# Which PSUM bank each of the last four output tiles takes

## The chip, the cores and the metric

The kernel runs on one core of one Trainium2 chip. The metric is the device time of one execution in microseconds (us). The time given is the median of three runs. One further execution was taken with the hardware profiler on; its rows are what is read below.

## The reference, cut to what matters

A block of attention feeds a feed-forward block (FFN). The attention keeps, for each of 768 positions, 96 local and 8 global keys. Its output is `x`, 3072 tokens by 512. The FFN takes the largest of three projections and projects back:

```
scores = scale * q @ k.T + bias            # (4, 8, 768, 64): batch, heads, positions, head size
a = softmax(where(keep, scores, -1e9));  attn = a @ v
x = attn.transpose(0, 2, 1, 3).reshape(3072, 512)
h = maximum(maximum(x @ w1, x @ w2), x @ w3)   # (3072, 768)
out = h @ w_out                                # (3072, 512), float32
```

## The kernel before, in words

**Tiles and chunks.** The 3072 tokens are 24 tiles of 128. The FFN works on chunks of two or four tiles (`SIZES`, line 88); the last chunk, number 6, has four tiles, 512 tokens. The hidden 768 columns are six blocks `f` of 128.

**Order.** The kernel is a list of small units written out by hand (`SCHEDULE`, lines 24 to 86). Every engine gets its instructions in that order and runs them in order; semaphores make it wait where it reads what another engine writes, or writes what another still reads. A unit's name is a letter and its numbers; `@n` gives the slot of a ring of buffers that it takes. Those that matter here:

- `Fc.f.j@n` (line 379): four matmuls of chunk `c`, block `f`, weight matrix `j`. The result is a 128 x 512 float32 tile `h` in slot `n` of the PSUM ring "h". The ring has four slots, each a bank.
- `fc.f.j` (lines 393 to 398) reads such a tile out: for `j` = 0 a copy into a bf16 tile `h01` (line 393), for `j` = 1 a maximum with it in place (line 395), for `j` = 2 the last maximum into slice `f` of the tile `ht` (line 398). With `.1` behind it, a `j` = 0 copy runs on VectorE (DVE); the maxima always do.
- `Oc.t` (line 403) is the second projection of one output tile: six matmuls, one for each `f`, that add up in one PSUM tile `po`, also in the ring "h". Each reads slice `f` of `ht` and slice `f` of `wo`.
- `wo` and the three `w123` tiles are filled earlier by casts, slice by slice (`W`, line 464, and `Q`, line 472).
- `E@2` (`u_E`) is the end: the second projection of the last chunk's four tiles, their copies out of PSUM (line 408, ScalarE, ACT, all but one) and their stores (line 409).

**The end.** `u_E` takes banks from the ring "h" six times through its helper `bank`. Tiles 0 and 1 get one bank each. TensorE (PE) runs blocks 0 to 4 of tile 0, then blocks 0 to 4 of tile 1, then block 5 of tile 0 and block 5 of tile 1. Tile 2 follows with all six blocks. Tile 3 comes in three pieces of 256, 128 and 128 columns, each in a bank of its own. That is 36 matmuls: 18 of 512 columns, 6 of 256 and 12 of 128. The stores of the first five results are issued by SyncE (SP), the last by ACT.

**The units just ahead.** The last of the schedule reads

```
s3.1 s5.0 s5.3 F6.2.2@2 F6.5.0@3 f6.4.2.1 f6.2.2.1 F6.0.2@1 f6.3.2.1 f6.0.2.1
F6.5.2@2 F6.5.1@0 f6.5.0.1@4 f6.5.1.1 f6.5.2.1 E@2
```

So when `u_E` begins, the four banks of the ring hold these tiles, in the order in which DVE reads them out: `F6.0.2` in bank 1, `F6.5.0` in bank 3, `F6.5.1` in bank 0, `F6.5.2` in bank 2. PE has computed `F6.5.2` ahead of `F6.5.1`, but DVE reads `F6.5.1` first. The slices 0 to 4 of `ht` are complete with the read-out of `F6.0.2`; slice 5 is complete with that of `F6.5.2`.

Before the change, `bank` counts on from the slot of `E@2`: its six calls give banks 2, 3, 0, 1, 2, 3.

Of the kernel before, what the change touches and what calls it, by code (L numbers as in the profile page):

```python
# [12 lines left out]
FP32 = mybir.dt.float32  # L13
# [73 lines left out]

SIZES = [4, 2, 2, 4, 4, 4, 4]
RINGS = {'r': 7, 'rv': 3, 'qb': 3, 'qkT': 4, 'sp': 2, 'h': 4, 'P': 8, 'xb': 4, 'xT': 3, 'wst0': 3, 'wst1': 3, 'ht': 2, 'h01': 5, 'rz': 4}


@with_exitstack
def kernel(
# [13 lines left out]
    nc = tc.nc  # L107
    B, H, S, D = q.shape
    NG = int(n_global)
# [4 lines left out]
    NT = S // 128  # L114
# [16 lines left out]
    pools = {}  # L131
    for name in RINGS:
        space = {"space": bass.MemoryType.PSUM} if name in ("sp", "h") else {}
# [3 lines left out]
    def ring(name, slot, shape, dtype, label):  # L137
        assert 0 <= slot < RINGS[name]
        return pools[name].tile(shape, dtype, name=label, tag=f"{name}{slot}")
# [22 lines left out]
    def words(ap):  # L162
        return ap.bitcast(mybir.dt.int32)
# [12 lines left out]
    def va(T):  # L176
        b, t = divmod(T, NT)
        return va_first[b % 2] if t == 0 else va_ring[(T - b - 1) % len(va_ring)]
# [88 lines left out]

    def u_V(slot, T, how):
        b, t = divmod(T, NT)
        for e in range(2):  # L270
            rows = slice(64 * e, 64 * e + NG // 2)
            if how == 2:
                copies[how](words(va(T)[rows]), words(va(b * NT)[rows]))  # L273
            else:
                copies[how](va(T)[rows], va(b * NT)[rows])
# [125 lines left out]
    def f2_mm(po, c, tt, fs, cols=slice(0, DM)):  # L401
        for f in fs:
            nc.tensor.matmul(po, ht[c][:, f, tt * 128:(tt + 1) * 128], wo[:, f, cols],  # L403
                             start=(f == 0), stop=(f == NF - 1))

    def f2_out(po, ost, c, tt, copy, cols=slice(0, DM), dma=nc.sync):
        T = chunks[c][tt]
        copy(ost, po)  # L408
        dma.dma_start(out=out[T * 128:(T + 1) * 128, cols], in_=ost)
# [14 lines left out]
    def u_E(slot):  # L424
        n = len(chunks[last])
        h, o = [0], [0]

        def bank(w):
            h[0] += 1
            return ring("h", (slot + h[0] - 1) % RINGS["h"], [128, w], FP32, "po")  # L430

        def stage(w):
            o[0] += 1
            name = ("wst0", "wst1")[o[0] % 2]
            return ring(name, o[0] // 2 % RINGS[name], [128, DM], FP32, "ost")[:, 0:w]

        po = [bank(DM) for _ in range(min(2, n - 1))]
        for tt, p in enumerate(po):
            f2_mm(p, last, tt, range(NF - 1))
        for tt, p in enumerate(po):  # L440
            f2_mm(p, last, tt, [NF - 1])
            f2_out(p, stage(DM), last, tt, nc.scalar.copy)
        for tt in range(2, n - 1):
            p = bank(DM)
            f2_mm(p, last, tt, range(NF))
            f2_out(p, stage(DM), last, tt, nc.scalar.copy)
        for lo, hi, copy, dma in ((0, 256, nc.scalar.copy, nc.sync), (256, 384, nc.vector.tensor_copy, nc.sync),
                                  (384, 512, nc.scalar.copy, nc.scalar)):
            p = bank(hi - lo)
            f2_mm(p, last, n - 1, range(NF), slice(lo, hi))  # L450
            f2_out(p, stage(hi - lo), last, n - 1, copy, slice(lo, hi), dma)
# [52 lines left out]
    def u_R(slot):  # L504
# [6 lines left out]
        nc.vector.tensor_copy(rbase[:, 0], rel[:, 1])  # L511

    units = {"l": u_l, "c": u_c, "v": u_v, "x": u_x, "y": u_y, "X": u_X, "G": u_G, "V": u_V, "S": u_S,
             "e": u_e, "m": u_m, "B": u_B, "K": u_K, "A": u_A, "n": u_n, "t": u_t, "u": u_u, "Z": u_Z,
             "F": u_F, "f": u_f, "O": u_O, "o": u_o, "s": u_s, "E": u_E, "w": u_w, "W": u_W, "q": u_q,
             "Q": u_Q, "D": u_D, "d": u_d, "R": u_R}
    with tc.manual_schedule():
        todo = SCHEDULE.split()
        for u in todo[:2] + [None] + todo[2:]:
# [3 lines left out]
            code, _, slot = u.partition("@")  # L523
# [34 lines left out]
```

## Time and profile before

| | |
|---|---|
| median of three runs | 179.37 us (179.29 to 179.99) |
| the profiled execution's own time | 179.93 us |
| its span, first to last instruction | 178.2 us |
| mean granted TensorE clock | 0.997 |
| PE busy with matmuls | 168.9 us, 95% of the span |
| DVE busy | 129.7 us, 73% |
| ACT busy | 107.6 us, 60% |
| second projection (line 403) | 34.0 us of PE, 156 matmuls |

The span is 1.73 us shorter than the execution's own time. In the profile's rows a group gives line, engine, operation, the tiles written and read, and a count; then busy time, the mean of one, and the idle time of the engine just ahead of them with what ended most of it. Rows of a timeline begin with the start and the duration in us. The chain of waits follows the last instruction back to whatever released each step. Matmuls are pipelined: one of 512 columns is shown as 0.38 us long while the next starts 0.216 us after it, so a run of n such matmuls shows as (n - 1) x 0.216 + 0.38 us.

### The profile page before, as it was taken

What the parts mean: (1) busy time and instruction counts of PE and PEld (TensorE: products, weight loads), DVE (VectorE), ACT (ScalarE), POOL (GpSimd) and SP (SyncE); (2) the same over time, 40 slices, a digit from 0 to 9 for tenths busy, and PEclk for the clock granted to TensorE, in tenths of its full rate; (3) what the DMA queues carried; (4) which work ended last, traced back from release to release, by engine and by line L of the source; (5) the groups of instructions that cost most, each with busy time, mean ns of one, the idle gap of its engine ahead of it and who ended that gap; (6) DMA issues with size and microseconds to landing.
All of it is one profiled execution on the core that took longest, in us unless ns stands there. A gap on an engine that the chain in (4) does not pass through costs nothing.

```text
span 178.2 us, 3903 instructions
## 1 busy us (share of the span) xinstructions
PE 168.9 (95%) x1525; PEld 94.6 (53%) x1525; DVE 129.7 (73%) x258; ACT 107.6 (60%) x166; POOL 45.6 (26%) x72
## 2 busy tenths in 40 slices
PE   7889999999999999999989999999999999999692
PEld 2456644567875867645345554644445464444242
DVE  6578849887787969576999568998668984355800
ACT  5988989666999768845759587426154823120022
POOL 3049755517053570000203601122001040000000
PEclk9999999999999999999999999999999999999998
DMA  4999999999999997499999899998980153460006
GB/s 144 351 292 314 365 371 323 342 297 332 299 263 130 163 259 144 91 347 290 198 314 224 155 162 289 269 147 257 219 169 3 42 137 60 177 235 0 4 21 216
DMA packets 66627, 37.49 MB, mean 210 GB/s; under 512 B 24624, under 2 KB 61360, under 8 KB 66608
## 3 DMA queue, kind: packets, MB, share of 16 engines
q1 hardware_dynamic: 66464, 37.17, 84.7%
q8 instruction: 12, 0.20, 0.4%
q10 hardware_dynamic: 144, 0.07, 0.1%
q14 instruction: 7, 0.06, 0.1%
HBM read 25.17 MB, written 6.29 MB: 177 GB/s over the span
## 4 chain that ended last, share of the span: by engine, by line
PE 77%; DMA 8%; ACT 5%; DVE 4%; issue 2%; POOL 1%; SPq 1%; ACTq 0%
PE h L379 45%; PE po L403 18%; PE sp L295 6%; DMA qkT<-qb 4%; DMA rawk<-in_k_dram 3%; PE op L337 3%; PE op L340 2%; ACT wmask L324 2%; ACT P L302 2%; PE tp L233 1%; PE tpq L227 1%; POOL va L273 1%; ACT qkT L241 1%; PE xtp L364 1%; SPq L195 1%
## 5 line engine op out<-in xcount | busy, mean ns | idle before, releaser
L379 PE MATMUL h<-xT,w 128*128 128x512 bf16 (+1 forms) x504 | 99.5, 349 | 0.1
L379 PEld LDWEIGHTS <-w 128*128 128x128 bf16 x504 | 47.3, 98 | 41.8 <-issue 0.7
L302 ACT ACTIVATE P<-sp 128x1024 bf16<-128x1024 f32 (+1 forms) x48 | 43.8, 953 | 14.7 <-PE sp L295 14.6
L403 PE MATMUL po<-wo,ht 128*128 128x512 bf16 (+2 forms) x156 | 34.0, 363 | 1.5 <-DVE ht L398 1.5
L395 DVE TENSOR_TENSOR h<-h,h 128x512 bf16<-128x512 bf16 (+1 forms) x42 | 25.0, 606 | 10.4 <-PE h L379 7.5
L311 DVE TENSOR_TENSOR P<-P,wmask 128x1024 bf16<-128x1024 bf16 x38 | 26.6, 708 | 7.9 <-ACT P L302 7.8
L398 DVE TENSOR_TENSOR ht<-h,h 128x512 bf16<-128x512 bf16 (+1 forms) x42 | 26.5, 644 | 4.4 <-PE h L379 3.4
L393 ACT CAST h<-h 128x512 bf16<-128x512 f32 (+1 forms) x24 | 12.7, 538 | 21.6 <-PE h L379 21.4
L213 POOL CAST va<-rawv 64x512 bf16<-64x512 f32 x20 | 15.1, 757 | 29.4 <-DMA rawv<-in_v_dram 19.2
L403 PEld LDWEIGHTS <-ht 128*128 128x128 bf16 x156 | 13.9, 98 | 15.8 <-DVE ht L398 2.0
L349 DVE TENSOR_TENSOR xb<-op,rz 128x512 bf16<-128x512 f32 x24 | 16.6, 691 | 0.8
L393 DVE CAST h<-h 128x512 bf16<-128x512 f32 (+1 forms) x18 | 10.7, 596 | 8.6 <-PE h L379 8.4
L295 PE MATMUL sp<-qkT 64*128 64x128 bf16 x352 | 14.5, 218 | 1.8 <-ACT qkT L241 0.8
L273 POOL COPY va<-vaf 4x260 int32<-4x260 int32 x20 | 9.1, 454 | 24.8 <-PE op L340 23.5
L295 PEld LDWEIGHTS <-qkT 64*128 64x128 bf16 x352 | 10.0, 94 | 10.0 <-issue 6.1
L418 ACT COPY ost<-po 128x512 f32<-128x512 f32 x15 | 8.8, 590 | 8.3 <-PE po L403 8.3
L337 PEld LDWEIGHTS <-P 128*128 128x128 bf16 x192 | 12.5, 97 | 2.5 <-issue 0.5
L337 PE MATMUL op<-va,P 128*128 128x65 bf16 x160 | 12.6, 193 | 0.0
L340 PEld LDWEIGHTS <-P 128*128 128x128 bf16 x160 | 10.5, 97 | 1.6
L478 PE MATMUL wp<-zeros 128*128 128x256 bf16 (+1 forms) x43 | 9.8, 360 | 1.2 <-DVE cap L496 1.2
L340 PE MATMUL op<-va,P 128*128 128x65 bf16 x128 | 9.9, 193 | 0.4 <-POOL va L273 0.4
L408 ACT COPY ost<-po 128x512 f32<-128x512 f32 (+2 forms) x5 | 2.3, 481 | 12.3 <-PE po L403 12.2
(69 smaller groups left out, 128.7 us busy)
## 6 DMA issues: line engine op xcount, KB each, us to landing
rawv<-in_v_dram SPq DMA_DIRECT2D x12, 512.0 KB, 7.5
out_dram<-ost SPq DMA_DIRECT2D x23, 256.0 KB, 2.5
rawk<-in_k_dram SPq DMA_DIRECT2D x10, 512.0 KB, 7.4
rawq<-in_q_dram SPq DMA_DIRECT2D x10, 512.0 KB, 7.3
wst<-in_moe_w_dram SPq DMA_DIRECT2D x3, 1024.0 KB, 10.3
wst<-in_moe_w_dram SPq DMA_DIRECT2D x3, 512.0 KB, 8.1
wost<-in_moe_w_out_dram SPq DMA_DIRECT2D x3, 512.0 KB, 6.5
rawqk<-in_k_dram SPq DMA_DIRECT2D x2, 512.0 KB, 5.0
```

The costliest lines, as they stand in the source:

```text
L213: copies[how](heads(va(T))[64 * e:64 * e + 64, :, 0:D], src)
L295: nc.tensor.matmul(sp[:, hh, j2, ds], qT(T - ds, 1)[hsl, jp], qT(T, 0)[hsl, jp], start=not how, stop=True, skip_group_check=True)
L302: nc.scalar.activation(P[:, :, 0:n], sps[T, g].rearrange("p a b d n -> p (a b) d n")[:, :, 0:n], AF.Exp, bias=0.0, scale=scale)
L311: mul(P, P, wmask[:, g, :, 0:2])
L337: nc.tensor.matmul(o, P[:, i, 0], heads(va(T))[:, h], start=True, stop=(t == 0), skip_group_check=True)
L340: nc.tensor.matmul(o, P[:, i, 1], heads(va(T - 1))[:, h], start=False, stop=True, skip_group_check=True)
L349: nc.vector.tensor_tensor(out=x.rearrange("p (g h) d -> p g h d", g=2), in0=o4[:, :, :, 0:64], in1=rz[:, :, :, None].to_broadcast([128, 2, ...
L379: nc.tensor.matmul(ps, w123[f // 2][:, j, dm, (f % 2) * 128:(f % 2) * 128 + 128], xT[c][:, dm], start=(dm == 0), stop=(dm == 3))
L393: copies[how](h01, ps)
L395: nc.vector.tensor_max(h01s[c, f], h01s[c, f], ps)
L398: nc.vector.tensor_max(dst, h01s[c, f].rearrange("p (t e i) -> p t e i", e=2, i=64), ps.rearrange("p (t e i) -> p t e i", e=2, i=64))
L403: nc.tensor.matmul(po, ht[c][:, f, tt * 128:(tt + 1) * 128], wo[:, f, cols], start=(f == 0), stop=(f == NF - 1))
```

## The change

`u_E` no longer counts on from its slot. Its calls of `bank` run through a fixed list of banks, 1, 3, 0, 2, and around again:

| | tile 0 | tile 1 | tile 2 | tile 3, columns 0 to 255 | 256 to 383 | 384 to 511 |
|---|---|---|---|---|---|---|
| before | 2 | 3 | 0 | 1 | 2 | 3 |
| changed | 1 | 3 | 0 | 2 | 1 | 3 |

```diff
+LAST_BANKS = (1, 3, 0, 2)
+
...
     def u_V(slot, T, how):
         b, t = divmod(T, NT)
+        if how == 3:
+            dst, src = (va(x).rearrange("(e i) w -> e i w", e=2)[:, 0:NG // 2] for x in (T, b * NT))
+            nc.sync.dma_start(out=dst, in_=src)
+            return
         for e in range(2):
...
         def bank(w):
             h[0] += 1
-            return ring("h", (slot + h[0] - 1) % RINGS["h"], [128, w], FP32, "po")
+            return ring("h", LAST_BANKS[(h[0] - 1) % len(LAST_BANKS)], [128, w], FP32, "po")
```

The new branch in `u_V` is for units `V` whose last number is 3. The schedule has sixteen units `V`, all with 0, 1 or 2 there, so the branch issues nothing. The schedule itself, the order of all instructions and the staging tiles of the output are as before.

## The prediction

> **What bounds the kernel now.** I read the page first, for the busy times and the costliest groups.
>
> ```profile
> PE 168.9 (95%) x1525; PEld 94.6 (53%) x1525; DVE 129.7 (73%) x258; ACT 107.6 (60%) x166; POOL 45.6 (26%) x72
> ...
> PE 77%; DMA 8%; ACT 5%; DVE 4%; issue 2%; POOL 1%; SPq 1%; ACTq 0%
> ...
> L403 PE MATMUL po<-wo,ht 128*128 128x512 bf16 (+2 forms) x156 | 34.0, 363 | 1.5 <-DVE ht L398 1.5
> ```
>
> PE is busy for 95% of the span and carries 77% of the chain, so time is won only where PE stands still. The second projection has 1.5 us of idle time ahead of it in all its 156 matmuls, and one releaser has ended all of that: DVE's last maximum into `ht`. To see where this is I took the chain of waits from 160 us to the end:
>
> ```profile
> 159.98 7.93 PE h L379 x36
> 167.91 0.02 issue
> 167.93 0.70 DVE h L395
> 168.63 0.02 issue
> 168.66 0.73 DVE ht L398
> 169.39 0.05 issue
> 169.44 5.40 PE po L403 x36
> 174.84 0.03 ACTq L408
> 174.86 0.04 issue
> 174.90 0.27 ACT ost L408
> ```
>
> It is one stop. PE finishes its last first-projection block at 167.91, then the chain leaves PE for two DVE instructions (`f6.5.1` and `f6.5.2`), and PE goes on at 169.44 with all 36 matmuls of `u_E` in a row. Nothing but PE and the last copy is on the chain from there on. The timeline of this stretch shows who is busy meanwhile:
>
> ```profile
> 166.21 0.73 DVE L398 TENSOR_TENSOR ht<-h,h 128x512 bf16<-128x512 bf16 x1
> 166.83 0.68 DVE L393 CAST h<-h 128x512 bf16<-128x512 f32 x1
> 167.93 0.69 DVE L395 TENSOR_TENSOR h<-h,h 128x512 bf16<-128x512 bf16 x1 [0.43 <-PE h L379]
> 168.66 0.72 DVE L398 TENSOR_TENSOR ht<-h,h 128x512 bf16<-128x512 bf16 x1
> ...
> 169.44 5.38 PE L403 MATMUL po<-wo,ht 128*128 128x512 bf16 x36 [1.54 <-DVE ht L398]
> 172.02 1.07 ACT L408 COPY ost<-po 128x512 f32<-128x512 f32 x2 [11.42 <-PE po L403]
> 172.63 2.84 SPq L409 DMA_DIRECT2D out_dram<-ost  x5
> ```
>
> By their order on DVE the four rows are the read-outs `f6.0.2` (bank 1, done at 166.94), `f6.5.0` (bank 3, 167.51), `f6.5.1` (bank 0, 168.62) and `f6.5.2` (bank 2, 169.38). The first matmul of `u_E` writes bank 2, which is the bank read out last.
>
> **The change part by part.** Nothing is added or removed: the same 36 matmuls, five ACT copies, one DVE copy and six stores. What moves is the time from which each bank may be written.
>
> *Start of tile 0.* Its bank is now 1, free at 166.94, almost a us before PE ends the last block. The matmuls of blocks 0 to 4 also need slices 0 to 4 of `ht`, complete at the same 166.94. The question is whether a matmul waits for its slice or for the whole tile `ht`, whose slice 5 comes at 169.38. In the row above both reasons (bank 2 and slice 5) end together, so it can't say. The timeline from 20.8 to 26.5 us can:
>
> ```profile
> 20.90 1.03 POOL L464 CAST w<-wst 128x1024 bf16<-128x1024 f32 x1 [0.23 <-DMA wst<-in_moe_w_dram]
> ...
> 22.80 1.03 POOL L464 CAST w<-wst 128x1024 bf16<-128x1024 f32 x1
> ...
> 23.37 3.40 PE L379 MATMUL h<-xT,w 128*128 128x512 bf16 x15
> ...
> 25.30 1.05 ACT L464 CAST w<-wst 128x1024 bf16<-128x1024 f32 x1
> ```
>
> These three casts fill the slices `j` = 1, 0 and 2 of one weight tile (`W0.1.2`, `W0.0.2`, `W0.2.0`), and all three stand ahead of `F0.0.1` in the schedule. `F0.0.1` reads slice 1 alone and starts at 23.37, before the second cast ends (23.83) and 1.9 us before the third begins. So a matmul waits for the slice it reads. `ht[:, f]` is cut in the same way.
>
> PE can therefore go straight on. A run of three matmuls takes 0.81 us on the timeline (shown length of the last 0.38, so 0.216 from start to start). The last of the 36 in the chain starts at 167.91 - 0.02 - 0.38 = 167.52 (nearly the end shown, less its length), so tile 0 starts at 167.52 + 0.22 = 167.73 instead of 169.44: **1.70 us earlier**. The idle time of 1.54 us is the lower bound of this; the other 0.16 is the pipelined part of the last matmul, 0.38 - 0.22, which the next one overlaps when nothing holds it.
>
> *Tile 1*, bank 3: free at 167.51, needed after five matmuls at 167.73 + 5 x 0.216 = 168.81. No wait. *Block 5 of tile 0* needs slice 5. PE comes to it after ten matmuls, 167.73 + 10 x 0.216 = 169.89. The slice was let go at 169.44 in the rows. Cover left: 0.45 us. This is the next thing that would be late; without it, each us that DVE takes longer is a us at the end. *Tile 2*, bank 0, is free at 168.62 and needed after 169.89. No wait.
>
> *Tile 3.* Its first piece takes bank 2, read out at 169.38 and needed some four us after PE's start. The second takes bank 1, the third bank 3, and there ACT's copies of tiles 0 and 1 must be over; before, the same two copies freed banks 2 and 3 for the same two pieces. They run from 172.02 to 173.09 (two in 1.07 us), and PE reaches these pieces 4.5 us after its start, at 173.98 (18 matmuls of 0.216, then 6 of half their width and half their time: 169.44 + 3.89 + 0.65). They move with the matmuls, so their 0.9 us of cover stays. No new wait.
>
> *What follows the matmuls.* ACT has been idle for 11.42 us before its first copy and DVE for 5.1 us before its one, so both can come 1.70 us earlier. SP's queue holds only these five stores; the view by stages gives a DMA share of 0.01 from 160 to 167.9 us and 0.00 up to 169.44, so the stores meet no other transfer. The closing part, 174.90 to 178.2 (last copy, store and the end of the program, 3.3 us), hangs on the last copy and moves whole.
>
> *Clock.* Whether the gap costs clock, or its end would give some back:
>
> ```profile
> 160.00:167.90 7.90, 7.89 (x36) 3.32 (x34) 5.21 (x8) 0.59 (x1) 0.00 (x0) 1.00 0.01 2
> 167.90:169.44 1.54, 0.00 (x1) 0.01 (x1) 1.41 (x2) 0.00 (x0) 0.00 (x0) 1.00 0.00 0
> 169.44:174.90 5.46, 5.38 (x36) 3.02 (x36) 0.29 (x1) 2.03 (x4) 0.00 (x0) 1.00 0.26 98
> ```
>
> The column behind the engines is the granted clock: 1.00 ahead of the gap, in it and after it. I put nothing for it. *The unused branch in `u_V`* issues nothing: 0.
>
> **The sum** is -1.70 us. The profiled execution would be 179.93 - 1.70 = 178.23 us, with a span of 176.5. The median of the runs is 0.56 us below that execution; the gap is at PE's end in either, so I take the same difference from the median: 179.37 - 1.70 = **177.67 us**, 0.95% less.
>
> **Rivals.** *1. No change.* The matmuls of blocks 0 to 4 still wait for slice 5, or the first bank was never what held them: 179.4 us. The row at 23.37 speaks against the first, the read-out order of the banks against the second. There is a more general form of it: the old order 2, 3, 0, 1 already goes through four banks, so that any order of them should do. The Trainium skill, Perfetto Trace Analysis, section Matmuls, says that independent matmul groups should go around the banks so that the read-out of one overlaps the next group. By that rule alone the change moves nothing, 0 in the sum; the trace agrees only in part, since the old order went around and still stood idle for 1.54 us. Chance 7%, together.
>
> *2. A part of it.* PE is let go not by `f6.0.2` but by a later read-out, say `f6.5.1` at 168.62 (its release some 0.06 later, like that of the last one: 169.44 - 169.38). Then PE starts at 168.68 and 0.76 us is won: 178.6. The wait would have to be put on the first matmuls for bank 0, which only tile 2 uses. Chance 4%.
>
> *3. Slower than before.* The place is DVE's last pair, `f6.5.1` and `f6.5.2`, which now runs beside ten matmuls that write PSUM and read `ht`, where PE used to stand still. If that slows the pair, slice 5 comes late. The cover is 0.45 us, the win 1.70, so it is slower from 2.15 us more on a pair that takes 169.38 - 167.93 = 1.45 us. If each took three times as long (+2.9): -1.70 + 2.9 - 0.45 = +0.75, 180.1 us. Against it: by lines, the 42 maxima into `h` take 0.69 us at most and the 42 into `ht` 0.74, nearly all of them beside a busy PE (100% from 100 to 160 us), and these two took 0.69 and 0.72 with PE idle. Chance 3%.
>
> **How the numbers follow.** My forecast has 86%. The range goes up to 178.5: the slowest run shown, 179.99, with the lower bound of the gain, 1.54, is 178.45. It goes down to 177.2: the fastest run, 179.29, less 1.70 is 177.59, and I add the 0.4 us that the runs spread on the other side. Rivals 1 to 3 lie outside, 14% in all. About 0.5% is what a measurement of this kernel can tell from no change: 0.9 us. The forecast lies under 178.5, so faster has 86%; rivals 1 and 2 (0 and -0.4%) make the same, 11%; rival 3 takes slower, 3%.
>
> **What would show it.** Right: the second projection's group has no idle time ahead of it; the chain goes from the 36 matmuls of line 379 to the 36 of line 403 without DVE between; the first of these starts at about 167.7, beside the rows of lines 395 and 398; ACT's first copy starts at about 170.3; span 176.5. Wrong: an idle time of 1.5 us by DVE that stays at the first matmul (rival 1), one of about 0.9 (rival 2), or one ahead of the eleventh matmul, with longer DVE rows (rival 3). Another execution whose earlier part, up to 167 us, runs some tenths of a us differently would shift the time without telling anything of the change.

## The result and the profile after

The changed kernel takes 178.15 us (median of 7 runs, 177.69 to 178.94), the kernel before, run beside it, 179.50 us (7 runs, 179.16 to 179.99). The ratio is 0.9927, 95% interval 0.9902 to 0.9953: faster by 0.5% to 1.0%. The profiled execution took 178.06 us with a span of 176.3 us.

The page's row of the second projection no longer names DVE. Of the 0.5 us of idle time left in the whole kernel, the stretch from 160 us on has 0.1, and a matmul without a record lies there (148 of the 156 have one):

```profile
L409 PE MATMUL po<-wo,ht 128*128 128x512 bf16 (+2 forms) x148 | 32.9, 362 | 0.5 <-issue 0.2
```

(The lines of the file have moved by 2 to 6: 379 is 385, 395 is 401, 398 is 404, 403 is 409, 408 is 414.) The chain of waits over the end, start and duration in us:

```profile
160.10 7.65 PE h L385 x34
167.75 3.24 PE po L409 x15
170.99 0.05 issue
171.04 1.93 PE po L409 x20
...
173.04 0.27 ACT ost L414
```

DVE has gone from it. PE's first projection runs straight into the second. (35 of the 36 matmuls have a record. The 0.05 us of "issue" is the place of the missing one: the matmuls on either side of it start two steps of 0.216 us apart.) The timeline of the same stretch:

```profile
167.58 5.37 PE L409 MATMUL po<-wo,ht 128*128 128x512 bf16 x35
167.78 0.69 DVE L401 TENSOR_TENSOR h<-h,h 128x512 bf16<-128x512 bf16 x1 [0.43 <-PE h L385]
168.51 0.73 DVE L404 TENSOR_TENSOR ht<-h,h 128x512 bf16<-128x512 bf16 x1
```

The two DVE rows that PE waited for now lie beside its matmuls. PE starts the second projection 0.20 us ahead of `f6.5.1` (167.58 against 167.78); before, it was 1.51 us behind it (169.44 against 167.93). The difference is 1.71 us.

**A yardstick that the earlier part doesn't move.** `f6.5.1` starts just after PE's last first-projection matmul, whatever the banks are. From there to the last copy of ACT is the stretch that the change can alter. Both are rows of every profile: before, 174.90 - 167.93 = 6.97 us; after, 173.04 - 167.78 = 5.26 us. That is 1.71 us less. The two profiled executions are 1.87 us apart (179.93 - 178.06); the rest, 0.15 us, is that `f6.5.1` starts at 167.78 in place of 167.93, in the part that the change doesn't touch. The experiments are read by the distance of the two rows, with the times beside it.

### The profile page after: what moved, and what is told of

It is laid out like the page before. It is cut to its first block, busy times and chain, and to the rows that moved or that the text cites. A ratio compares the mean times of both kernels' runs of the same rounds, so it can differ in the third digit from the quotient of the medians.

```text
span 176.3 us, 3882 instructions
## 1 busy us (share of the span) xinstructions
PE 166.8 (95%) x1504; PEld 94.3 (53%) x1525; DVE 131.2 (74%) x258; ACT 107.6 (61%) x166; POOL 46.1 (26%) x72
## 4 chain that ended last, share of the span: by engine, by line
PE 77%; DMA 8%; ACT 5%; DVE 5%; issue 2%; POOL 1%; ACTq 0%
PE h L385 45%; PE po L409 18%; PE sp L301 6%; DMA qkT<-qb 4%; DMA rawv<-in_v_dram 4%; PE op L343 2%; PE op L346 2%; ACT wmask L330 2%; ACT P L308 2%; DVE xb L355 1%; PE tp L235 1%; POOL va L279 1%; DVE ht L404 1%; PE xtp L370 1%; PE tpq L229 1%
## 5 line engine op out<-in xcount | busy, mean ns | idle before, releaser
L385 PE MATMUL h<-xT,w 128*128 128x512 bf16 (+1 forms) x491 | 98.5, 348 | 1.1 <-issue 0.2
L409 PE MATMUL po<-wo,ht 128*128 128x512 bf16 (+2 forms) x148 | 32.9, 362 | 0.5 <-issue 0.2
L317 DVE TENSOR_TENSOR P<-P,wmask 128x1024 bf16<-128x1024 bf16 x38 | 27.9, 742 | 7.1 <-ACT P L308 7.0
```

The source lines that it names most:

```text
L317: mul(P, P, wmask[:, g, :, 0:2])
L385: nc.tensor.matmul(ps, w123[f // 2][:, j, dm, (f % 2) * 128:(f % 2) * 128 + 128], xT[c][:, dm], start=(dm == 0), stop=(dm == 3))
```

## The experiments

The theory: PE starts a tile of the end as soon as that tile's own bank has been read out and the slices of `ht` that it reads are written. Where PE comes later than that, nothing is lost. The rivals: any rotation of the banks is as good as another; the exact match of the whole order counts; a matmul waits for all of `ht`; there is no cover behind slice 5; or part of the difference has nothing to do with the change. The four kernels on banks share 26 runs of the kernel before (179.82 us), the other four share another 26 (179.63 us).

| kernel | median, us | ratio (95% interval) | expected ratio | `f6.5.1` to last copy, us | less than before | expected |
|---|---|---|---|---|---|---|
| before | 179.82 / 179.63 | 1 | | 6.97 | | |
| again | 178.17 | 0.9910 (0.9880 to 0.9940) | 0.9905 | 5.25 | 1.72 | 1.70 |
| rot3 | 178.33 | 0.9922 (0.9894 to 0.9949) | 0.9905 | 5.25 | 1.72 | 1.70 |
| rot1 | 178.76 | 0.9942 (0.9917 to 0.9967) | 0.9940 | 5.89 | 1.08 | 1.07 |
| rot0 | 179.13 | 0.9960 (0.9937 to 0.9984) | 0.9958 | 6.19 | 0.78 | 0.76 |
| whole | 178.87 | 0.9940 (0.9911 to 0.9968) | 0.9940 | 5.89 | 1.08 | 1.07 |
| after_x1 | 178.37 | 0.9916 (0.9888 to 0.9943) | 0.9919 | 5.53 | 1.44 | 1.45 |
| after_x3 | 179.81 | 1.0004 (0.9979 to 1.0029) | 1.00 | 6.98 | -0.01 | about 0 |
| before_x1 | 180.91 | 1.0072 (1.0037 to 1.0106) | 1.0039 | 7.69 | -0.72 | -0.70 |

Expected ratios other than that of `again` are 1 less the expected us over the median of before, 179.5. From `before` to `rot0` the rows differ in the banks alone (`again` also has the unused branch in `u_V`, the rotations don't).

**again**: the changed kernel, not edited.

> The changed kernel once more, beside the three other orders of banks, on the same chip. Theory (release): tile 0 of the last chunk starts when its own bank has been read out and the slices of ht that it reads are written; with bank 1 that is before PE needs it. No idle time ahead of the first matmul of line 409, 1.70 us won, ratio 0.9905. Rival (elsewhere): part of the difference is an earlier start of the whole stretch, unconnected with the change; then the ratio is nearer 1 than 0.9905 in time while the gap in the rows is closed all the same.

It took 178.17 us, and its rows repeat the first profile: 173.42 - 168.17 = 5.25. By time the win is 1.65 us here (179.82 - 178.17) and 1.35 in the first comparison, with 1.72 and 1.71 in the rows; the intervals, 1.08 to 2.16 and 0.84 to 1.76 us, hold the values of the rows. The stretch starts later here than in the profile before (168.17 against 167.93), not earlier, so nothing supports the rival that a part of the win is an earlier start.

**rot3**: the old code, the last unit's slot changed.

```diff
-    F6.5.2@2 F6.5.1@0 f6.5.0.1@4 f6.5.1.1 f6.5.2.1 E@2
+    F6.5.2@2 F6.5.1@0 f6.5.0.1@4 f6.5.1.1 f6.5.2.1 E@3
```

> The old rotation, begun one bank on: banks 3, 0, 1, 2, 3, 0 in place of 2, 3, 0, 1, 2, 3. Release theory: tile 0's bank 3 is free before PE's last block ends; tile 1's bank 0 is free at 168.68 on the clock of the profile before, and PE needs it at 168.81, 0.13 us later: no idle time, the whole 1.70 us, same as the changed kernel (177.7). Rival (the match of the whole order counts): tile 1's bank comes late by the 0.7 us of one more read-out, so about 1.0 us is won (178.4). Rival (any rotation is as good): no gain, 179.4.

The second projection's row in its timeline up to 170 us:

```profile
167.78 2.54 PE L403 MATMUL po<-wo,ht 128*128 128x512 bf16 x11
```

Eleven matmuls in 2.54 us is 10 x 0.216 + 0.38: none of them waited, though tile 1 took bank 0, whose read-out ended 0.19 us before PE came to it (`f6.5.1` runs from 167.98 for 0.69 us, to 168.67; PE's sixth matmul starts at 167.78 + 5 x 0.216 = 168.86). So the match of the whole order isn't needed. One digit in the schedule gives the same as the change, and without the unused branch.

**rot1**: the same edit with `E@1`; **rot0**: with `E@0`.

> The old rotation begun at bank 1: 1, 2, 3, 0, 1, 2. Release theory: tile 0 starts at once, but tile 1 takes bank 2, released at 169.44, while PE could write it at 168.81: PE idles for 0.63 us between the fifth and the sixth matmul, so 1.70 - 0.63 = 1.07 us is won (178.3). Rival (only the first bank counts): 1.70 us. Rival (any rotation is as good): 0.

> The old rotation begun at bank 0: 0, 1, 2, 3, 0, 1. Release theory: tile 0 waits for the third of the four read-outs, released at 168.68, so PE starts 0.76 us earlier than before and 0.95 us later than in the changed kernel; nothing after that waits. 0.76 us won (178.6). Rival (any rotation is as good, or all but the old one): 0, or the whole 1.70.

The timeline of `rot1`, up to 170 us:

```profile
167.62 1.24 PE L403 MATMUL po<-wo,ht 128*128 128x512 bf16 x5
...
169.32 1.04 PE L403 MATMUL po<-wo,ht 128*128 128x512 bf16 x4 [0.46 <-DVE ht L398]
```

and of `rot0`, up to 170 us:

```profile
167.75 0.69 DVE L395 TENSOR_TENSOR h<-h,h 128x512 bf16<-128x512 bf16 x1 [0.43 <-PE h L379]
...
168.49 1.67 PE L403 MATMUL po<-wo,ht 128*128 128x512 bf16 x7 [0.78 <-DVE h L395]
```

In `rot1` five matmuls of tile 0 run, then PE stands still until `f6.5.2` has read out tile 1's bank 2. In `rot0` it is the first matmul that waits, and now for `f6.5.1`, which reads bank 0: another releaser (line 395 in place of 398) and half the idle time. All four rotations, the old one among them, are cases of one rule, each to within 0.02 us, and the four are not alike, so "any rotation" is out.

**whole**: the changed kernel, with tile 0 and tile 1 each run through.

```diff
         for tt, p in enumerate(po):
-            f2_mm(p, last, tt, range(NF - 1))
-        for tt, p in enumerate(po):
-            f2_mm(p, last, tt, [NF - 1])
+            f2_mm(p, last, tt, range(NF))
             f2_out(p, stage(DM), last, tt, nc.scalar.copy)
```

> The changed kernel, with all six blocks of tile 0 run in a row and then all six of tile 1, instead of five, five, one, one. Release theory by slices: only the sixth matmul needs slice 5 of ht, released at 169.44 on the clock of the profile before; PE comes to it at 167.73 + 5 x 0.216 = 168.81 and idles for 0.63 us there: 1.07 us of the gain stays (178.3). Rival (wait for the whole tile ht): the first matmul waits, nothing is won (179.4). Rival (the bank alone counts, the slices never end a wait): no idle time, the whole 1.70 us.

```profile
168.37 1.24 PE L409 MATMUL po<-wo,ht 128*128 128x512 bf16 x5
...
169.30 0.72 DVE L404 TENSOR_TENSOR ht<-h,h 128x512 bf16<-128x512 bf16 x1
...
170.08 1.25 PE L409 MATMUL po<-wo,ht 128*128 128x512 bf16 x5 [0.46 <-DVE ht L404]
```

The banks are the new ones here, and still 0.63 us are lost. Five matmuls run ahead of the end of `f6.5.2` (170.02), the sixth behind it. So a matmul waits for its own slice of `ht`, not for the tile, and the order five, five, one, one is the other part of the gain: it gives DVE ten matmuls of time for slice 5 instead of five. That order was in the kernel before as well. It could do nothing there, because the bank held the first matmul back until slice 5 was there anyway. (The chain of waits of `whole` reaches the last copy through a store, which lets it go at 174.41 us. PE's last matmul ends at 174.38 as shown, and the copy starts 0.08 us behind it, in `rot1` 0.09: the store costs nothing to be seen.)

**after_x1** and **after_x3**: the changed kernel with the maximum of `f6.5.1` done two or four times (the values stay the same); **before_x1**: the kernel before with it done twice.

```diff
-    F6.5.2@2 F6.5.1@0 f6.5.0.1@4 f6.5.1.1 f6.5.2.1 E@2
+    F6.5.2@2 F6.5.1@0 f6.5.0.1@4 f6.5.1.1 f6.5.1.1 f6.5.2.1 E@2
```

> The changed kernel with the maximum of f6.5.1 done twice on DVE (the second changes no value), so that slice 5 of ht comes about 0.70 us later. Theory (cover of 0.45 us): PE idles for 0.70 - 0.45 = 0.25 us ahead of the eleventh matmul of the end; 0.25 us slower than the changed kernel, 1.45 us faster than before. Rival (no cover: slice 5 ends a wait already): 0.70 us slower than the changed kernel. Rival (cover larger than thought): nothing.

> The same maximum done four times, three more than in the changed kernel: slice 5 comes about 2.1 us later. Theory: idle time of 2.1 - 0.45 = 1.65 us ahead of the eleventh matmul, the whole gain is gone, within 0.1 us of the kernel before. This is the point from which a slower pair on DVE would have made the change a loss. Rival (no cover): 2.1 us slower than the changed kernel, 0.4 us slower than before.

> The kernel before with the maximum of f6.5.1 done twice. Theory: DVE's pair was on the path there without any cover, so the whole 0.70 us is added: the gap ahead of line 403 grows from 1.54 to 2.24 us, 0.4% slower than before. Rival (the gap is set by something other than DVE's last pair): no change.

`after_x1`, `after_x3` and `before_x1` in that order, by their timelines:

```profile
167.71 3.47 PE L409 MATMUL po<-wo,ht 128*128 128x512 bf16 x14
167.91 1.41 DVE L401 TENSOR_TENSOR h<-h,h 128x512 bf16<-128x512 bf16 x2 [0.43 <-PE h L385]
169.35 0.73 DVE L404 TENSOR_TENSOR ht<-h,h 128x512 bf16<-128x512 bf16 x1
170.13 0.76 PEld L409 LDWEIGHTS <-ht 128*128 128x128 bf16 x5 [0.60 <-DVE ht L404]
```

```profile
167.60 2.32 PE L409 MATMUL po<-wo,ht 128*128 128x512 bf16 x10
167.80 2.85 DVE L401 TENSOR_TENSOR h<-h,h 128x512 bf16<-128x512 bf16 x4 [0.43 <-PE h L385]
170.69 0.72 DVE L404 TENSOR_TENSOR ht<-h,h 128x512 bf16<-128x512 bf16 x1
...
171.47 0.82 PE L409 MATMUL po<-wo,ht 128*128 128x512 bf16 x3 [1.55 <-DVE ht L404]
```

```profile
169.40 5.38 PE L403 MATMUL po<-wo,ht 128*128 128x512 bf16 x36 [2.27 <-DVE ht L398]
```

In the changed kernel `f6.5.2` starts 0.73 us behind `f6.5.1` (168.51 - 167.78). In `after_x1` it is 1.44 us, 0.71 later, and the end comes 0.27 later (5.53 - 5.26). In `after_x3` it is 2.89 us, 2.16 later, and the end 1.72 later. Both leave a cover of **0.44 us**. Exactly ten matmuls run ahead of the stop in `after_x3`, so it is block 5 of tile 0 that waits. In `before_x1` the same extra maximum costs its whole 0.72 us: no cover there. By time `before_x1` lost 1.28 us (180.91 against 179.63), more than the 0.72 of its rows. The rest goes with the granted clock of its runs. In five of the twelve its mean was 0.990 or 0.991, and these took 181.69 to 182.79 us. In the other seven it was 0.999 or 1.0, as in the profiled one, and their median is 180.38 us: 0.75 above 179.63, close to the 0.72 of the rows. Why the clock was lower in those five stays open; in no other run here whose clock is on record was it below 0.996.

## Why the prediction was right

- **Start of tile 0, 1.70 us.** Right: 1.71 in the rows. The lower bound, the idle time shown of 1.54 us, would have been too small by 0.17, about the 0.16 us by which matmuls overlap. The prediction's working has a slip of 0.01: 167.91 - 0.02 - 0.38 is 167.51, and from its start at 167.73 to 169.44 it is 1.71, as measured.
- **Wait by slice, not by tile.** Read from the weight casts at 20.90 to 26.35 us; `whole` shows it directly for `ht`.
- **Tile 1 and tile 2 wait for nothing.** Right: no idle time in the row of 35, and it is 5.37 us long where the 36 before took 5.38. `rot1` shows what it costs when tile 1's bank is late: 0.63 us.
- **Cover of block 5, 0.45 us.** Right: 0.44 by two experiments.
- **Copies, stores and the closing part move whole.** Right: from the start of the last copy to the end of the span it is 3.3 us in both (178.2 - 174.90, 176.3 - 173.04).
- **Rival 1 (no change)** falls with the profile after; as "any rotation" with `rot0` and `rot1`. The rule that the prediction weighed (the Trainium skill, Perfetto Trace Analysis, section Matmuls) asks that groups go around the banks and says nothing of where to begin. The beginning alone is worth 0 to 1.72 us in the four rotations here.
- **Rival 2 (a part)** doesn't hold for the change, but its price does: it is `rot0`, 0.78 us in the rows against 0.76.
- **Rival 3 (slower DVE pair)** falls: beside PE the two took 0.69 and 0.73 us, with PE idle 0.69 and 0.72. Its point of decision, 2.15 us more on DVE, was right: `after_x3`, with 2.16 more, ends level with the kernel before (1.0004).
- **The time.** 178.15 us against 177.67 forecast. Of the 0.48 us, 0.13 is the base: with more runs the kernel before has 179.50, not 179.37. The other 0.35 lies within the spread of the runs (177.69 to 178.94), and the forecast ratio, 0.9905, within the interval. Two of the seven runs lie above the forecast range. In all eight comparisons (the first one, and every kernel of the table but `before_x1`) less is won by time than by the rows, by 0.02 to 0.36 us. They share three sets of runs of the kernel before, and each interval holds the value of the rows, so whether a little of the gain is lost ahead of the stretch isn't shown. That the profiled execution came out under its forecast (178.06 us against 178.23) is luck: its earlier part ran 0.15 us shorter. The 0.4 us by which the prediction stretched its range downwards as the runs' spread is in no row: the three runs lay 0.62 us above their median and 0.08 below.

## What to carry to other kernels

When a stage hands a ring of PSUM banks to the next, list the banks in the order in which they are read out and let the next stage begin with the one that is free first; later ones need only be free by the time that PE comes to them. Then look at what else the first instructions read: a free bank wins all of its time only if the data behind the last read-out is needed late, so put the work that doesn't need it first (`whole` left this out and kept 1.08 of 1.71 us). A gain of this kind is the time from one start to the next less the usual step, which is more than the idle time shown (1.71 against 1.54 us).

## What was not expected

**The time of the part ahead varies almost as much as the gain.** `f6.5.1` starts at 167.17 us in the profile of `before_x1` and at 168.57 in that of `whole`, though all the work ahead of it is the same. So `before_x1` has a span of 178.1 us, no longer than that of the kernel before (178.2), with 0.72 us more in its end. Compared with the kernel before by DVE's instructions one by one, both are within 0.03 us of it at 76 us; from 103 us on, `whole` is 0.63 us behind and `before_x1` 0.76 ahead, and neither moves by more than 0.02 from there up to 165 us. In between, the chain of waits of two of the three passes through a transposing DMA that SP issues into `qkT`. Of the kernel before:

```profile
81.81 7.91 DMA qkT<-qb
...
89.76 0.62 PE sp L295 x16
```

and of `whole`:

```profile
82.79 7.56 DMA qkT<-qb
...
90.40 0.62 PE sp L301 x16
```

PE's scores start right behind it, 0.64 us later in `whole`; in `before_x1` they start at 88.98, 0.78 us earlier, and the chain stays on PE there. Ahead of that transpose SP issues two loads of `q`, which take it 3.36 us in the kernel before (from 78.28) and 4.87 in `whole` (from 77.75). In `before_x1` they take 3.38 us, much as before, but SP comes to them 0.77 us earlier (77.51). So the issues themselves are longer in `whole` alone. What makes SP's issues come earlier or take longer in one execution than in another was not tried. A single span is no measure of a change of this size; a distance between two rows inside the changed stretch is.

**A stop of PE that the rows don't show as idle time.** In `after_x1` PE lost 0.27 us ahead of the eleventh matmul, and the timeline still merges 14 matmuls without a gap. The sign is the length: 3.47 us in place of 13 x 0.216 + 0.38 = 3.19, and the weight load's row, which begins anew after 0.60 us of idle time that DVE ended.
